# Sequence tails four tokens to a partition, turned by one-hot matmuls, with casts and copies dealt out anew

## The chip, the cores and the metric

The kernel runs on one core of one Trainium2 chip. Five engines take part, each with its own instruction stream: TensorE (matmuls, called PE in the profile, its weight loads PEld), VectorE (DVE), ScalarE (ACT), GpSimd (POOL) and SyncE (SP), whose stream issues all transfers that matter here. Work done by one engine and needed by another is handed over by semaphores. The metric is the device time of one execution in microseconds; three runs of the kernel before took 306.62, 306.86 and 310.41 us, and their median, 306.86, is the time to which the change is compared.

## The reference

Eight sequences of 576 tokens pass through attention with 8 heads of 64 in which a token sees only tokens at most 32 away, and then, all 4608 tokens together, through two layers with a squared rectifier between them:

```python
B, H, S, D = q.shape                                   # 8, 8, 576, 64
scores = np.matmul(q, k.transpose(0, 1, 3, 2)) / np.sqrt(D)
scores = np.where(np.abs(pos[:, None] - pos[None, :]) <= 32, scores, -1e9)
attn = np.exp(scores - np.max(scores, axis=-1, keepdims=True))
attn = attn / (np.sum(attn, axis=-1, keepdims=True) + 1e-09)
x = np.matmul(attn, v).transpose(0, 2, 1, 3).reshape(B * S, H * D)
r = np.maximum(x @ w_in, 0.0)                          # 512 -> 2048
return (s * (r * r) + b) @ w_out                       # 2048 -> 512
```

Inputs and output are float32; the kernel multiplies in bfloat16.

## The kernel before

**Attention.** A sequence has nine tiles of 64 tokens. Two neighbouring tiles make a unit; a unit's scores are taken transposed (keys on partitions, a window of 128 queries beside them), ScalarE takes the exponential out of PSUM, VectorE multiplies by a mask of ones and zeros, and TensorE multiplies by V, to which a column of ones is added for the row sums. `finish` divides (VectorE) and brings the result X into the array `xt`, with the model dimension on partitions: for the first units (number below `XPE`, line 913) by four transposes on TensorE and a copy on ScalarE (line 923), for the later ones by a DMA that transposes, issued on SP (line 932).

**Q and K.** For that, Q and K must lie with head dimension on partitions. For sequences 0 to 2 the first 512 tokens are loaded four tokens to a partition, in runs of 1 KB, cast, and turned on TensorE. The last 64 tokens, the tail ("t"), are loaded apart in `part` (line 701): one token to a partition, Q on partitions 0 to 63 and K on 64 to 127, in runs of 256 bytes, one per token and head. The tail is cast (line 691), turned by four 128x128 transposes (line 705) into a PSUM bank of W, AVN or SC, and two copies on ScalarE (line 696) take Q and K out. Sequences 3 to 7 are loaded by `piece` (lines 752, 759), cast on GpSimd (line 778) and turned by DMA (line 794); they are treated as one long sequence, `LONG`.

**V** is loaded by SP (line 605) and cast at line 614, by GpSimd for sequence 1 and by VectorE from sequence 2 on; sequence 0 has paths of its own (`spread_runs`).

**The layers.** Tokens go through in blocks of 512; `SPLIT` cuts blocks 0, 1 and 2 into smaller ones. `s1` is the first layer: matmuls into one of two halves of PSUM bank W (line 1147), the rectifier on ScalarE (line 1154), the square on VectorE (line 1160). `second` is the second layer of a block in seven products instead of eight (line 1204), for which VectorE forms sums and differences of the weights (line 1176) and of the squared activations (line 1196), and adds up the results (line 1220). `constant` puts the term of b through w_out (line 1279). Weights are loaded in sixteen pieces (line 577) and cast by GpSimd (line 580).

**PSUM** has four banks of two halves here: W, O, SC, AVN. `av_banks` says in which one a unit's attention-times-V and the transposes of its X are put; `late_scores` (lines 984 and 987) takes the scores of sequence 0's last tile, which need the tail.

**What sets the order.** The program is built as a graph of tasks, each with an engine, an estimated cost, a key (due time, small is early) and the buffers that it reads and writes. `plan` goes through it with a model of the engines and of the DMA rings and writes out one fixed order per engine; transfers of the first three sequences and of the weights are chained in the order of `ORDER0`, `ORDER1` and `ORDER2`. So an estimate, a key or an engine that changes can move other tasks, also far away. `stir` (line 659) adds matmuls whose result nobody reads, a number of times by `STIR`.

Of the kernel before, what the change touches and what calls it, by code (L numbers as in the profile page):

```python
# [11 lines left out]
S = 576  # L12
# [19 lines left out]
SPLIT = {0: (224, 128, 160), 1: (256, 256), 2: (256, 256)}  # L32
FIRST = ((0, 0), (1, 0), (0, 1), (2, 0), (1, 1), (2, 1), (0, 2), (1, 2), (2, 2), (0, 3), (1, 3), (2, 3))
WOUTE = (("pool", "pool"),) * 4
# [5 lines left out]
XPE = 25  # L40
# [9 lines left out]
EV0 = ("act", "dve", "act", "dve", "pool")  # L50
BANK1 = ("O", "AVN", "SC", "O", "AVN")
EV1 = ("pool", "pool", "pool", "pool", "pool")
EV2 = ("dve",) * 5
# [3 lines left out]
        ("turn", 3, "q"): 1, ("turn", 3, "k"): 1, ("scores", 2): 1, ("scores", 3): 1, ("av", 0): 5}  # L57
# [266 lines left out]
def bass_sliding_window_symmetric__then__act_starrelu_kernel(  # L324
# [23 lines left out]
    with ExitStack() as es:  # L348
# [332 lines left out]
        def part(b, which, load_key, key, banks, slack):  # L681
# [4 lines left out]
            res, tile = banks[take("bank", len(banks))]  # L686
            tile = tile.bitcast(BF16)
# [11 lines left out]
            if which == "t":  # L699
                stg, stgr = stage(DM)  # L700
                add("sp", [lambda e, src=src, p0=p0: e.dma_start(
                    stg[p0:p0 + 64, :].rearrange("p (h d) -> p h d", h=H), src[b, :, 512:S, :].rearrange("h p d -> p h d"))
                    for src, p0 in ((q, 0), (k, 64))], 1000.0, writes=stgr, key=load_key, dma=("l", 64, 27.0))
                cast(nat[:, 0:DM], stg, DM, stgr)
                add("pe", [lambda e, a=a: e.transpose(tile[:, 128 * a:128 * a + 128], nat[:, 128 * a:128 * a + 128], IDENT[:, :])
                           for a in range(NPAIR)], 300.0, reads=natr + ["IDENT"], writes=[res], key=key)
                view = tile[:, 0:512].rearrange("p (a c) -> p a c", a=NPAIR)
                for name, dst, c0 in (("QT", QT[slot][:, :, WIN + 512:WIN + S], 0), ("KT", KT[slot][:, :, 512:S], 64)):
                    leave(dst, view[:, :, c0:c0 + 64], 256, [(name, slot, NTILE - 1, pr) for pr in range(NPAIR)])
                return  # L710
# [151 lines left out]
        def av_banks(b, u):  # L862
            name = ("SC", "O", "SC", "O", "AVN")[u] if b == 0 else BANK1[u] if b == 1 else "AVN"
# [34 lines left out]
        def finish(b, u, key=None):  # L898
# [14 lines left out]
            if n < XPE:  # L913
# [8 lines left out]
                for a0, a1 in zip(cuts, cuts[1:]):  # L922
                    add("act", lambda e, a0=a0, a1=a1: e.copy(  # L923
                        XT[:, :, a0 % XR:a0 % XR + a1 - a0], view[:, :, p0 + a0 - x0:p0 + a1 - x0]),
                        190 + 0.833 * 4 * (a1 - a0), reads=avr, writes=xt_res(a0, a1), key=key)
# [635 lines left out]
```

## Time and profile before

| what | value |
|---|---|
| median of three runs | 306.86 us |
| the profiled execution | 308.19 us |
| its span, first to last instruction | 306.3 us |
| mean granted TensorE clock | 0.994 |
| busy: TensorE, VectorE, ScalarE, GpSimd | 295.7, 237.2, 157.3, 66.6 us |
| moved by DMA | 54.31 MB |

The span is that of the profiled execution; what lies around it is in that execution's own time. Busy shares are means over stages that have different limits, so the stretches of the span are read one by one. TensorE's matmuls are pipelined: a single matmul's duration holds a drain that overlaps the next one, and what a matmul costs in a row of them is the duration of the row divided by their number.

### The profile page before, as it was taken

To read this page: it belongs to the slowest core of one execution; us is meant where nothing else is said; L and a number is where in the kernel's file an instruction comes from. 1 tells how busy PE (TensorE), PEld (TensorE's weight loads), DVE (VectorE), ACT (ScalarE), POOL (GpSimd) and SP (SyncE) were. 2 spreads that over 40 slices of the span, in tenths; PEclk is the share of its full clock that TensorE was granted. 3 is DMA by queue.
4 is the path that set the end of the run, shared out by engine and by line. 5 is a ranking of instruction groups with operands and counts; after the bars stand their busy time and mean duration, and the time that the engine had idled before them with its cause. 6 is when DMAs were issued, how large, how long until landed. Compare 5 with 4: busy or idle time off the path is not lost.

```text
span 306.3 us, 8830 instructions
## 1 busy us (share of the span) xinstructions
PE 295.7 (97%) x3851; PEld 212.3 (69%) x3851; DVE 237.2 (77%) x409; ACT 157.3 (51%) x246; POOL 66.6 (22%) x78
## 2 busy tenths in 40 slices
PE   8989999899999999999999999998999999999994
PEld 3458777698888887567666675665666666666783
DVE  4666888899879796999799888897867776566673
ACT  3746975684877563655555345543454433333200
POOL 5155577200000360046024400460000000000000
PEclk9979999999999999999999999999999999999999
DMA  7999999999992997999799779997803111200223
GB/s 208 306 254 313 315 287 354 274 260 238 179 216 67 251 209 148 279 234 188 187 242 184 145 178 253 185 169 136 235 20 88 54 47 35 69 34 2 70 72 107
DMA packets 118073, 54.31 MB, mean 177 GB/s; under 512 B 90688, under 2 KB 113856, under 8 KB 118032
## 3 DMA queue, kind: packets, MB, share of 16 engines
q1 hardware_dynamic: 118032, 53.72, 75.6%
q8 instruction: 31, 0.51, 0.8%
q14 instruction: 10, 0.08, 0.1%
HBM read 36.70 MB, written 9.44 MB: 151 GB/s over the span
## 4 chain that ended last, share of the span: by engine, by line
PE 73%; DMA 17%; SPq 3%; POOL 3%; DVE 1%; ACT 1%; issue 0%; POOLq 0%
PE o L1204 31%; PE w L1147 30%; DMA stg<-in_moe_w_out_dram 5%; DMA stg<-in_k_dram 4%; PE avn L884 3%; DMA stg<-in_q_dram 3%; DMA stg<-in_moe_w_in_dram 3%; PE sc L1204 2%; POOL nat L778 2%; SPq L759 2%; PE sc L826 2%; DMA kt<-nat 2%; PE avn L915 1%; POOL wout L580 1%; PE avn L718 1%; ACT ex L1005 1%
## 5 line engine op out<-in xcount | busy, mean ns | idle before, releaser
L1147 PE MATMUL w<-xt,win 128*128 128x512 bf16 (+4 forms) x832 | 144.6, 316 | 0.3 <-issue 0.3
L1154 ACT ACTIVATE r<-w 128x512 bf16<-128x512 f32 (+2 forms) x148 | 86.4, 587 | 97.5 <-PE w L1147 96.0
L1147 PEld LDWEIGHTS w<-xt,win 128*128 128x128 bf16 x832 | 74.9, 99 | 34.4 <-issue 1.3
L1160 DVE TENSOR_TENSOR gt<-r 128x1024 bf16<-128x1024 bf16 (+3 forms) x100 | 62.1, 628 | 23.8 <-ACT r L1154 23.1
L1204 PE MATMUL o<-wout,gt 128*128 128x256 bf16 x528 | 66.4, 273 | 0.0
L1204 PEld LDWEIGHTS o<-wout,gt 128*128 128x128 bf16 x528 | 51.0, 98 | 12.7
L778 POOL CAST nat<-stg 128x1024 bf16<-128x1024 f32 (+2 forms) x28 | 33.8, 1207 | 78.4 <-DMA stg<-in_q_dram 62.4
L854 ACT ACTIVATE ex<-sc 128x1024 bf16<-128x1024 f32 (+1 forms) x29 | 29.7, 1023 | 15.7 <-PE avn L884 13.2
L1204 PE MATMUL o<-tw,gt 128*128 128x256 bf16 x272 | 34.6, 273 | 0.0
L1220 DVE SCALAR_TENSOR_TENSOR outs<-o,sb,cvec 128x512 f32<-128x512 f32 (+1 forms) x36 | 25.8, 717 | 8.1 <-PE o L1204 7.8
L1204 PEld LDWEIGHTS o<-tw,gt 128*128 128x128 bf16 x272 | 26.3, 98 | 7.2
L1220 DVE SCALAR_TENSOR_TENSOR outs<-o,sb,outs 128x512 f32<-128x512 f32 (+1 forms) x27 | 19.2, 713 | 7.1 <-PE o L1204 7.0
L1196 DVE TENSOR_TENSOR gt<-gt 128x1024 bf16<-128x1024 bf16 (+1 forms) x26 | 24.4, 940 | 0.3
L858 DVE TENSOR_TENSOR ex<-ex,mask 128x1024 bf16<-128x1024 bf16 (+1 forms) x29 | 22.1, 762 | 1.5 <-ACT ex L854 0.8
L908 DVE TENSOR_TENSOR xn<-avn,rec 128x512 bf16<-128x512 f32 (+1 forms) x31 | 21.3, 686 | 0.5
L884 PE MATMUL avn<-vb,ex 64*64 64x65 bf16 x944 | 19.9, 197 | 1.4 <-DMA kt<-nat 1.2
L884 PEld LDWEIGHTS avn<-vb,ex 64*64 64x64 bf16 x944 | 12.9, 106 | 10.6 <-issue 5.5
L1204 PE MATMUL o<-tw,gsum 128*128 128x256 bf16 x136 | 17.7, 273 | 0.0
L1204 PEld LDWEIGHTS o<-tw,gsum 128*128 128x128 bf16 x136 | 13.0, 98 | 3.7
L614 DVE CAST vb<-vst 128x512 bf16<-128x512 f32 (+1 forms) x28 | 13.8, 498 | 1.6 <-DMA vst<-in_v_dram 1.6
L1196 DVE TENSOR_TENSOR gsum<-gt 128x1024 bf16<-128x1024 bf16 x18 | 13.6, 758 | 0.3
L923 ACT COPY xt<-avn 128x512 bf16<-128x512 bf16 (+2 forms) x19 | 10.0, 533 | 5.1 <-PE avn L915 5.0
(130 smaller groups left out, 228.6 us busy)
## 6 DMA issues: line engine op xcount, KB each, us to landing
out_dram<-outs SPq DMA_DIRECT2D x32, 256.0 KB, 3.1
vst<-in_v_dram SPq DMA_DIRECT2D x28, 256.0 KB, 4.9
stg<-in_k_dram SPq DMA_DIRECT2D x24, 256.0 KB, 6.7
stg<-in_q_dram SPq DMA_DIRECT2D x5, 1024.0 KB, 6.8
stg<-in_moe_w_in_dram SPq DMA_DIRECT2D x8, 512.0 KB, 8.2
stg<-in_moe_w_out_dram SPq DMA_DIRECT2D x8, 512.0 KB, 7.6
stg<-in_q_dram SPq DMA_DIRECT2D x4, 512.0 KB, 8.4
stg<-in_k_dram SPq DMA_DIRECT2D x4, 512.0 KB, 8.3
```

The costliest lines, as they stand in the source:

```text
L614: (lambda e: e.tensor_copy(VB[0:n, vb, :, 0:D], VST[0:n, vs, :, :])),
L778: (lambda e, dst=dst, src=src: e.tensor_copy(dst, src)),
L854: add("act", lambda e, dst=flat_dst, src=flat_src: e.activation(dst, src, AF.Exp, bias=0.0, scale=0.125), 190 + 0.833 * 512 * len(hs), rea ...
L858: add("dve", lambda e, flat=flat, mask=mask: e.tensor_tensor(flat, flat, mask, ALU.mult), 130 + 0.53 * 512 * len(hs), reads=[("E", ei, hp, ...
L884: return [lambda e: e.matmul(av[64 * x:64 * x + 64, h, 0:D + 1], lhsT=buf[64 * g:64 * g + 64, h % 2, h // 2, c:c + 64], rhs=VB[64 * g:64 * ...
L908: add("dve", lambda e: e.tensor_tensor(XN[xi][0:p1, :].rearrange("p (a c) -> p a c", a=H), av[0:p1, :, 0:D], REC[ri][0:p1, :].rearrange("p ...
L1147: add("pe", [lambda e, g=g, kc=kc: e.matmul(wt[:, g, :], lhsT=WIN_BF[:, kc, (f0 + g) * 128:(f0 + g + 1) * 128], rhs=XT[:, kc, t0 % XR:t0 % ...
L1154: add("act", lambda e: e.activation(rt, wt, AF.Relu, bias=0.0, scale=1.0), 190 + 0.833 * ng * nt, reads=[("W", wb)], writes=[("R1", rb, ha ...
L1160: add("dve", lambda e: e.tensor_tensor(GT[gs][:, f1:f1 + nf, g0:g0 + nt], rr, rr, ALU.mult), 130 + 0.55 * nf * nt, reads=[("R1", rb, x) fo ...
L1196: add("dve", lambda e: e.tensor_tensor(dst, x, y, op), 1240.0 if half is None else 690.0, reads=reads, writes=writes, key=k)
L1204: add("pe", [lambda e, g=g, j=j, dst=dst: e.matmul(dst, lhsT=lhs[:, g, 128 * j:128 * j + 128], rhs=rhs[:, g, :], start=first and g == 0 an ...
L1220: add("dve", lambda e, src=src, dst=dst, other=other: e.scalar_tensor_tensor(dst, src, SB128[:, 0:1], other, ALU.mult, ALU.add), 200 + 1.0 ...
```

## The change

1. The tail's load: its tokens lie four to a partition (partition = head and group of four tokens), Q in the first 256 columns and K in the next, in runs of 1 KB. It is turned by 16 matmuls against columns picked from the identity, each for one of the four tokens or K's four, and one half of the heads, into float32 PSUM; the two copies out undo the order.
2. Engines: from sequence 2 on, V is cast on ScalarE and VectorE in turn, ScalarE first in each sequence. The last piece of w_out is cast by VectorE. Of sequence 0's five copies of X, the second is done by VectorE.
3. Banks and waits of sequence 0: unit 2 uses AVN and not SC, and no longer waits for unit 0's transposes; the late scores use W and not AVN.
4. Three matmuls whose result nobody reads are added behind unit 2's transposes of sequence 0.
5. Block 3 is cut into two halves of 256 tokens.
6. `XPE` is 23 and not 25: two units of X more are turned by DMA.

```diff
-SPLIT = {0: (224, 128, 160), 1: (256, 256), 2: (256, 256)}
+SPLIT = {0: (224, 128, 160), 1: (256, 256), 2: (256, 256), 3: (256, 256)}
-WOUTE = (("pool", "pool"),) * 4
+WOUTE = (("pool", "pool"),) * 3 + (("pool", "dve"),)
-XPE = 25
+XPE = 23
+COPY0 = ("act", "dve", "act", "act", "act")
-EV2 = ("dve",) * 5
+EV2 = ("act", "dve", "act", "dve", "act")
-        ("turn", 3, "q"): 1, ("turn", 3, "k"): 1, ("scores", 2): 1, ("scores", 3): 1, ("av", 0): 5}
+        ("turn", 3, "q"): 1, ("turn", 3, "k"): 1, ("scores", 2): 1, ("scores", 3): 1, ("av", 0): 5, "late": 3}
...
-                add("sp", [lambda e, src=src, p0=p0: e.dma_start(
-                    stg[p0:p0 + 64, :].rearrange("p (h d) -> p h d", h=H), src[b, :, 512:S, :].rearrange("h p d -> p h d"))
-                    for src, p0 in ((q, 0), (k, 64))], 1000.0, writes=stgr, key=load_key, dma=("l", 64, 27.0))
+                add("sp", [lambda e, src=src, c0=c0: e.dma_start(
+                    stg[:, c0:c0 + 256], src[b, :, 512:S, :].rearrange("h (s i) d -> h s (i d)", i=4))
+                    for src, c0 in ((q, 0), (k, 256))], 1000.0, writes=stgr, key=load_key, dma=("l", 16, 50.0))
...
-                add("pe", [lambda e, a=a: e.transpose(tile[:, 128 * a:128 * a + 128], nat[:, 128 * a:128 * a + 128], IDENT[:, :])
-                           for a in range(NPAIR)], 300.0, reads=natr + ["IDENT"], writes=[res], key=key)
+                tile = wide
+                pick = IDENT.rearrange("p (a x s) -> p x a s", a=NPAIR, x=2)
+                add("pe", [lambda e, i=i, hp=hp: e.matmul(
+                    tile[64 * hp:64 * hp + 64, 64 * i:64 * i + 64].rearrange("p (a s) -> p a s", a=NPAIR),
+                    lhsT=nat[:, 64 * i:64 * i + 64], rhs=pick[:, hp, :, :], start=True, stop=True)
+                    for i in range(8) for hp in (0, 1)], 400.0, reads=natr + ["IDENT"], writes=[res], key=key)
...
-            name = ("SC", "O", "SC", "O", "AVN")[u] if b == 0 else BANK1[u] if b == 1 else "AVN"
+            name = ("SC", "O", "AVN", "O", "AVN")[u] if b == 0 else BANK1[u] if b == 1 else "AVN"
...
+                    if n < len(COPY0) and COPY0[n] == "dve":
+                        add("dve", lambda e, dst=dst, src=src: e.tensor_copy(dst, src),
+                            60 + 1.04 * 4 * (a1 - a0), reads=avr, writes=xt_res(a0, a1), key=key)
...
-                        AVN[0:64, hp, pr * 128:pr * 128 + 128], lhsT=KT[0][p, pr, 64 * x:64 * x + 64],
+                        W[0:64, hp, pr * 128:pr * 128 + 128], lhsT=KT[0][p, pr, 64 * x:64 * x + 64],
...
-                land["av", 0, u] = pe_part(-25.0 + u, av=av_part(0, u), waits=[land["xt", u - 2]] if u > 1 else [])
+                land["av", 0, u] = pe_part(-25.0 + u, av=av_part(0, u), waits=[land["xt", u - 2]] if u > 2 else [])
                 finish(0, u, -25.0 + u)
+            stir("late", ("SC", 0), SC[:, 0, :], EARLY + 0.45, [land["xt", 2]])
```

More of the change, by code (lines that the diff above doesn't have):

```diff
@@ L685, in part @@
             nat, natr = NAT[ni], [("NAT", ni)]
-            res, tile = banks[take("bank", len(banks))]
-            tile = tile.bitcast(BF16)
+            res, wide = banks[take("bank", len(banks))]
+            tile = wide.bitcast(BF16)
             eng, out_eng = FCAST[which] if b < 2 else "act", FOUT[which]
```

21 lines of the change are left out of this document (11 added, 10 removed).

## The prediction

> **What bounds the kernel now.** I read the page's head first, then the same span cut into stretches (columns: stretch, its length, busy time of TensorE, its weight loads, VectorE, ScalarE and GpSimd with counts, granted TensorE clock, DMA share, GB/s).
>
> ```profile
> span 306.3 us, 8830 instructions
> PE 295.7 (97%) x3851; PEld 212.3 (69%) x3851; DVE 237.2 (77%) x409; ACT 157.3 (51%) x246; POOL 66.6 (22%) x78
> 6.00:20.00 14.00, 12.13 (x210) 6.30 (x208) 8.10 (x15) 8.36 (x15) 4.24 (x6) 0.99 1.12 300
> 20.00:24.00 4.00, 3.92 (x72) 3.14 (x70) 2.85 (x5) 2.54 (x6) 2.28 (x3) 0.60 1.18 213
> 24.00:55.00 31.00, 29.64 (x571) 24.10 (x571) 24.57 (x47) 22.06 (x41) 20.86 (x22) 1.00 1.10 316
> 55.00:58.00 3.00, 2.05 (x21) 1.40 (x19) 1.86 (x4) 1.57 (x3) 1.11 (x2) 1.00 1.15 273
> 58.00:205.00 147.00, 147.00 (x2087) 109.64 (x2085) 128.61 (x212) 87.19 (x130) 34.43 (x30) 1.00 0.98 203
> 205.00:210.00 5.00, 3.84 (x35) 2.06 (x35) 3.84 (x6) 1.83 (x4) 0.00 (x0) 1.00 0.97 188
> 210.00:302.30 92.30, 92.20 (x885) 64.24 (x885) 63.75 (x103) 31.84 (x50) 0.00 (x0) 1.00 0.25 71
> ```
>
> The reader is to see two kernels in one. From 58 us TensorE is full: 147.00 of 147.00, 3.84 of 5.00, 92.20 of 92.30. Before 58 us it isn't: it lacks 14.00 − 12.13 = 1.87, 0.08, 1.36 and 0.95 us, and between 20 and 24 us it had 0.60 of its clock. There the DMA share is above 1 in every stretch. So the first 58 us are held by what the DMA engines bring and by the chains from it to TensorE; after that, only TensorE's own work counts, and one gap near 208 us. All that this change can win lies in about 4 us of early idle time, the slow stretch, and that gap. The waits of TensorE name two of them:
>
> ```profile
> PE avn L884 <- DMA kt<-nat: 1.2, 1, 1.2
> PE sc L1279 <- POOL wout L580: 1.0, 1, 1.0
> 19.00:20.00 1.00, 0.84 (x24) 0.54 (x21) 0.07 (x1) 1.00 (x4) 0.75 (x1) 0.90 1.12 199
> 20.00:21.00 1.00, 0.92 (x41) 0.66 (x36) 0.00 (x0) 1.00 (x3) 0.29 (x1) 0.50 1.07 214
> 23.00:24.00 1.00, 1.00 (x23) 0.86 (x24) 0.96 (x3) 0.43 (x2) 0.49 (x1) 0.89 1.15 195
> ```
>
> The last three rows show the clock fall to 0.50 late in the microsecond from 19 and come back within the one from 23: about 0.2 + 3 + 0.2 = 3.4 us at half clock, behind a stretch in which TensorE idled. That costs up to 1.7 us.
>
> **The start: sequence 0 (clock, bank and copy edits).** The timeline there (start, duration, engine, line; in brackets the idle time before):
>
> ```profile
> 18.56 0.40 PE L705 MATMUL w<-ident,nat 128*128 128x128 bf16 x4 [0.76 <-POOL nat L691]
> 19.89 0.62 ACT L923 COPY xt<-o 128x512 bf16<-128x512 bf16 x1
> 20.07 0.94 PE L884 MATMUL sc<-vb,ex 64*64 64x65 bf16 x32
> 20.37 1.44 ACT L997 ACTIVATE ex<-avn 64x1024 bf16<-64x1024 f32 x2
> 20.95 2.79 PE L1147 MATMUL w<-xt,win 128*128 128x224 bf16 x16
> 21.07 0.21 DVE L906 RECIPROCAL rec<-sc 128x8 f32<-128x8 f32 x1 [2.00 <-PE sc L884]
> 26.52 0.93 PE L1147 MATMUL w<-xt,win 128*128 128x224 bf16 x8
> ```
>
> TensorE waits 0.76 us for the tail's cast, and only later runs unit 2's attention-times-V (0.94 us), since that shares bank SC with unit 0. In bank AVN, and without the wait for unit 0's transposes, it can run inside the 0.76. Unit 1's copy (0.62 on ScalarE, ahead of the exponentials) goes to VectorE, idle for 2.00 us just then, so the late exponentials (1.44) may begin up to 0.62 sooner. Against that, the late scores move from AVN to W, the bank of the first layer: its first matmuls, now begun at 20.95 beside the exponentials, must wait for their end. That is the wait added; behind it on TensorE stands everything of the first layer, and ScalarE and VectorE wait for that in turn. The exponentials end at 20.37 + 1.44 = 21.81, or 21.2 with the copy gone: a start 0.25 to 0.9 later. The 16 matmuls took 2.79 at half clock; at full clock, from 0.93 for eight, about 1.7. So they would end between 21.2 + 1.7 = 22.9 and 21.8 + 1.7 = 23.5 where they ended at 23.74: 0.2 to 0.8 won if the clock holds, up to 0.9 lost if it doesn't. With the attention already done elsewhere I take **−0.6** (ends −1.7 and +0.9).
>
> The three added dummy matmuls, by the five of line 659 below, take 3 × 0.22 = 0.65; they are to fall in the wait for bank W, so most is hidden: **+0.1** (0 to 0.65 if that cover is gone).
>
> **The tails.** One tail is 128 KB of Q and 128 KB of K. The rows are of the timeline, of a stretch, and of the DMA issues (KB each, us to landing):
>
> ```profile
> 14.55 1.25 PE L659 MATMUL sc<-onesw 128*128 128x512 bf16 x5
> 25.00:30.00 5.00, 5.00 (x78) 4.32 (x70) 3.11 (x7) 3.36 (x8) 2.48 (x3) 1.00 1.11 344
> stg<-in_q_dram SPq DMA_DIRECT2D x8, 128.0 KB, 5.3
> 47.87 0.40 PE L1279 MATMUL sc<-wout,onesw 128*32 128x512 bf16 x4
> 28.88 0.61 PE L718 MATMUL avn<-ident,nat 128*128 128x128 bf16 x8
> ```
>
> Now they come in runs of 256 bytes, afterwards of 1 KB. The trace has no row for one form alone; the nearest are two stretches with the DMA full, one in which sequence 1's tail is under way (213 GB/s, 20 to 24 us), one mostly of long runs (344, from 25 us). 262 KB take 1.23 us at the one and 0.76 at the other: 0.47 a tail, 0.94 for the two tails that ORDER0 and ORDER1 issue ahead of the last w_out load. SP also waits for free staging, so not all of it arrives: **−0.4** (ends −0.9 and 0, below it in the first rival). SP issues two transfers per tail, as now.
>
> On TensorE, 16 one-hot matmuls of 64 columns replace 4 transposes, which took 0.40 with their drain (18.56 us above). Four of 32 weight columns and 512 run in 0.40, not four times that: column halves run side by side. Eight pairs of 64 columns then stream in 8 × 0.03 = 0.2, within the same 0.4; one after the other it is 0.6. I take +0.1 a tail, **+0.3** (0 to +0.75). ScalarE's two copies out move as many elements and stay.
>
> **The last w_out piece.** It is cast by VectorE, not GpSimd. Three rows of the timeline, and one of the groups for the new price:
>
> ```profile
> 56.08 1.04 POOL L580 CAST wout<-stg 128x1024 bf16<-128x1024 f32 x1 [1.01 <-DMA stg<-in_moe_w_out_dram]
> 57.15 2.36 DVE L1176 TENSOR_TENSOR tw<-wout 128x2048 bf16<-128x2048 bf16 x2 [1.14 <-POOL wout L580]
> 57.17 0.40 PE L1279 MATMUL sc<-wout,onesw 128*32 128x512 bf16 x4 [0.95 <-POOL wout L580]
> L691 DVE CAST nat<-stg 128x1024 bf16<-128x1024 f32 x2 | 1.4, 694 | 1.2 <-DMA stg<-in_k_dram 1.2
> ```
>
> 1.04 becomes 0.69, and TensorE waited for its end: **−0.35**. VectorE idles 1.14 there, so nothing is queued behind it; if it were late, squares of the first layer would wait. Only 0.95 can be won here by all terms together, unless TensorE itself arrives earlier, which the first part provides.
>
> **Block 3 in halves, V casts, two units by DMA.** Rows of the chain that ended last (start, duration), of the groups by form (count, busy and mean, idle before), of two lines of DMA issues, and of the timeline:
>
> ```profile
> 65.32 0.87 PE w L1147 x8
> 120.24 0.86 PE w L1147 x4
> L1160 DVE TENSOR_TENSOR gt<-r 128x1024 bf16<-128x1024 bf16 x48 | 37.1, 774 | 18.6 <-ACT r L1154 18.1
> L1160 DVE TENSOR_TENSOR gt<-r 128x512 bf16<-128x512 bf16 x36 | 18.5, 524 | 3.4 <-ACT r L1154 3.3
> L614 DVE CAST vb<-vst 128x512 bf16<-128x512 f32 x26 | 13.0, 505 | 1.6 <-DMA vst<-in_v_dram 1.6
> L668 ACT CAST nat<-stg 128x512 bf16<-128x512 f32 x1 | 0.6, 618 | 1.6 <-DMA stg<-in_q_dram 1.6
> L932 SPq DMA_TRANSPOSE xt<-xn x14: 1181/1259/3060, 175.0 to 245.8; - x14
> 168.11 1.78 SPq L794 DMA_TRANSPOSE kt<-nat  x1
> DMA to landing us min/median/max: 2.3/4.6/6.5
> 176.41 0.40 PE L826 MATMUL sc<-qt,kt 64*64 64x128 bf16 x16
> ```
>
> Eight matmuls of 256 take 0.87, four of 512 take 0.86: 16 such groups, +0.16 on TensorE. VectorE squares 16 × 0.524 − 8 × 0.774 = +2.2 us, ScalarE the same elements. Of 28 V casts 16 go to ScalarE: VectorE −8.1, ScalarE +9.9. Between 58 and 205 us VectorE has 147 − 128.6 = 18 us free, ScalarE 60, and TensorE is full: **0**. A cast that waits for its load would hold the rectifiers queued behind it on ScalarE, and TensorE with them; VectorE waited 1.6 us for such loads in all, and that is the bound.
>
> Two units lose 4 matmuls of 128 each on TensorE, 8 × 0.05 (eight transposes took 0.61 above, four 0.40) = −0.4, and ScalarE two copies. With the split's +0.16, **−0.25**. They add two DMA transposes to SP, 1.26 to 3.06 us each, ahead of sequence 6's loads and transposes. Sequence 6's main K transpose, issued at 168.11, lands 4.6 later by the median, 172.7, and is used at 176.41: 3.7 of cover for 2 × 1.26 = 2.5. So nothing, in my sum; the gap near 208 us is fed by sequence 7, 30 us on, and I leave it at its 1.2 (it may close or double).
>
> **Sum.** −0.6 + 0.1 − 0.4 + 0.3 − 0.35 − 0.25 = −1.2 us. The profiled execution took 308.19 (306.33 of span, 1.86 around it) and would take 307.0. The median of the runs shown is 306.86, 1.33 below the profiled one; I can't see whether those runs had the slow stretch at all, so I count half of the −0.6: 306.86 − 0.9 = 306.0. **I forecast 306.0 us**, 305.2 to 306.6 for this case.
>
> **Rivals.**
>
> *Half the engines.* The new source runs over 8 heads, then 16 groups of four tokens; if the transfer is dealt out by the outer 8, it uses 8 engines, at half of 344 GB/s: 262 KB take 1.52 us, 0.29 worse than now. For two tails +0.6 in place of −0.4: 307.0. For it: nothing in the trace shows a load with an outer count of 8. Against it: other engines' packets overlap. [...] Chance 0.2.
>
> *SP is late for sequence 6 (slower).* If the two X transposes cost SP the longest seen, 2 × 3.06 = 6.1, the 3.7 of cover fails and TensorE stands 2.4 us at 176: 306.0 + 2.4 = 308.4. It decides from 1.85 us a transpose. For it: one of 14 took 3.06, and SP's loads there wait on a full DMA. Against: the median of 1.26. Chance 0.2.
>
> *The clock.* The half-clock stretch stays or moves behind the wait for bank W: +0.9 in place of the counted −0.3: 307.2. For it: the first layer begins later. [...] Chance 0.15.
>
> *Both gaps close.* The start gains 1.7 in place of 0.3 and 208 us its 1.2: 303.4 at best, 304.5 at half of it. Chance 0.1.
>
> **How the numbers follow.** Forecast 0.35. The range takes in the rivals: 304.2 (half of the best case) to 308.9 (the late transposes with some of the clock's loss). Two per cent, about what a measurement of this kernel tells from no change, is 6 us: below 300.7 no case lies, above 313.0 only an order of queues gone wrong in several places. Faster 0.01, within 0.96, slower 0.03.
>
> **What would show it.** The clock row at 1.00 from 20 to 24 us; first-layer matmuls starting past 21.2; the wait at line 1279 under 0.6; tail loads landing sooner than the 5.3 of their row; 16 matmuls of a tail in 0.4 to 0.6; VectorE near 231 us and ScalarE near 167; no new TensorE wait near 176. A new TensorE wait of over a microsecond after 58 us would make me wrong, as would tails landing later.

## The result and the profile after

The changed kernel took 308.02 us (median of 22 runs, 307.15 to 310.35), the kernel before 306.64 (22 runs beside them on the same chip, 305.03 to 311.31). The ratio is 1.0052 with a 95% interval of 1.0033 to 1.0070; when the changed kernel was run again on another chip (median 308.56, there against 307.68) it was 1.0030 [1.0002, 1.0058]. Weighted by the two intervals that is 1.0045, or 1.4 us slower. The forecast was 306.0, a gain of 0.9. The ratios here and below compare undisturbed runs alone (all or nearly all of a kernel's, but nine of twelve and six of twelve for two of the kernels with sixteen groups outermost, whose other runs took 313.8 to 315.3), so they needn't be the quotient of two medians. A tenth of a per cent is 0.31 us.

The profiled execution after took 307.18 us. The page's head:

```profile
span 305.4 us, 9028 instructions
PE 291.9 (96%) x3924; PEld 217.1 (71%) x3946; DVE 236.1 (77%) x403; ACT 164.1 (54%) x259; POOL 63.9 (21%) x77
```

The stretches (their length, busy time of TensorE, its weight loads, VectorE, ScalarE, GpSimd, granted clock, DMA share, GB/s):

```profile
6.00:20.00 14.00, 11.50 (x240) 5.92 (x238) 8.69 (x17) 7.88 (x14) 3.89 (x6) 1.00 1.09 307
20.00:24.00 4.00, 3.53 (x72) 2.11 (x68) 2.75 (x6) 2.67 (x5) 2.56 (x4) 1.00 1.10 272
24.00:55.00 31.00, 28.80 (x543) 24.05 (x544) 25.30 (x47) 21.67 (x40) 20.48 (x22) 1.00 1.06 318
55.00:58.00 3.00, 2.87 (x39) 1.96 (x38) 3.00 (x5) 2.39 (x6) 0.00 (x0) 1.00 1.07 274
205.00:210.00 5.00, 4.95 (x35) 3.20 (x33) 4.46 (x7) 2.33 (x4) 0.87 (x2) 1.00 0.96 184
```

In this execution three losses of before are gone: the clock is 1.00 from 20 to 24 us (it was 0.60), the gap at the w_out wait is nearly closed (2.87 of 3.00, where it was 2.05), and so is the gap near 208 us (4.95 of 5.00, where it was 3.84). But TensorE now lacks 2.50, 0.47 and 2.20 us in the first three stretches, where it lacked 1.87, 0.08 and 1.36. TensorE's waits (in total, times, longest):

```profile
PE w L708 <- POOL nat L692: 1.2, 1, 1.2
...
PE avn L920 <- DVE xn L913: 1.0, 1, 1.0
...
PE o L889 <- POOL vb L615: 0.9, 1, 0.9
```

The wait for the tail's cast grew from 0.76 to 1.2 us, and the waits for K at 208 us (1.2) and for w_out (1.0) have gone, but one for X near 142 us (1.0) and one for a cast of V near 44 us (0.9) have come. In this pair of executions, what was won was given back elsewhere. The wait for the tail's cast is a poor measure of the two kernels, though: it was 2.0 us in a second trace of the changed kernel, and 1.8 and 2.5 in two traces of a kernel that has before's order on TensorE (only w_out's last cast is moved, below).

The two profiled executions are a poor pair for the size of it: before's was 1.55 us above its kernel's median and had the stretch of half clock, after's is 0.84 below its own and hasn't. In one execution of the changed kernel the second layer began at 59.96 us and in another at 61.34, so what follows goes by ratios of many runs for the size, and by traces for the place. The clock of the profiled pair isn't that of the mean either: the granted clock, as the mean over the span, was 0.9940 over 152 executions of the kernel before, 0.9933 over the 22 of the changed kernel and 0.9939 over 12 more. On the mean the change won nothing of it.

### The profile page after: what moved, and what is told of

Its sections match the earlier page's. It is cut to its first block, busy times and chain, and to the rows that moved or that the text cites. A ratio compares the mean times of both kernels' runs of the same rounds, so it can differ in the third digit from the quotient of the medians.

```text
span 305.4 us, 9028 instructions
## 1 busy us (share of the span) xinstructions
PE 291.9 (96%) x3924; PEld 217.1 (71%) x3946; DVE 236.1 (77%) x403; ACT 164.1 (54%) x259; POOL 63.9 (21%) x77
## 4 chain that ended last, share of the span: by engine, by line
PE 83%; DVE 5%; DMA 4%; SPq 3%; ACT 2%; issue 2%; POOL 1%; POOLq 0%
PE w L1157 37%; PE o L1214 34%; PE avn L889 4%; PE sc L831 2%; PE sc L1214 2%; DMA stg<-in_moe_w_in_dram 2%; DMA stg<-in_k_dram 2%; DVE gt L1170 1%; SPq L651 1%; PE avn L920 1%; DVE gsum L1206 1%; SPq L621 1%; SPq L578 1%; ACT r L1164 1%; DVE gt L1206 1%
## 5 line engine op out<-in xcount | busy, mean ns | idle before, releaser
L1157 PE MATMUL w<-xt,win 128*128 128x256 bf16 (+4 forms) x874 | 139.7, 301 | 2.5 <-issue 1.0
L1157 PEld LDWEIGHTS w<-xt,win 128*128 128x128 bf16 x896 | 80.6, 98 | 31.3 <-issue 1.0
L1170 DVE TENSOR_TENSOR gt<-r 128x512 bf16<-128x512 bf16 (+3 forms) x108 | 65.6, 614 | 25.8 <-ACT r L1164 24.8
L783 POOL CAST nat<-stg 128x1024 bf16<-128x1024 f32 (+2 forms) x28 | 32.4, 1158 | 82.4 <-DMA stg<-in_q_dram 67.9
L889 PE MATMUL avn<-vb,ex 64*64 64x65 bf16 x976 | 20.6, 197 | 0.4
L1206 DVE TENSOR_TENSOR gsum<-gt 128x1024 bf16<-128x1024 bf16 x18 | 15.0, 832 | 0.3
L911 DVE RECIPROCAL rec<-avn 128x8 f32<-128x8 f32 (+1 forms) x32 | 6.5, 202 | 8.9 <-PE avn L889 8.9
```

The source lines that it names most:

```text
L783: (lambda e, dst=dst, src=src: e.tensor_copy(dst, src)),
L889: return [lambda e: e.matmul(av[64 * x:64 * x + 64, h, 0:D + 1], lhsT=buf[64 * g:64 * g + 64, h % 2, h // 2, c:c + 64], rhs=VB[64 * g:64 * ...
L1157: add("pe", [lambda e, g=g, kc=kc: e.matmul(wt[:, g, :], lhsT=WIN_BF[:, kc, (f0 + g) * 128:(f0 + g + 1) * 128], rhs=XT[:, kc, t0 % XR:t0 % ...
L1170: add("dve", lambda e: e.tensor_tensor(GT[gs][:, f1:f1 + nf, g0:g0 + nt], rr, rr, ALU.mult), 130 + 0.55 * nf * nt, reads=[("R1", rb, x) fo ...
L1206: add("dve", lambda e: e.tensor_tensor(dst, x, y, op), 1240.0 if half is None else 690.0, reads=reads, writes=writes, key=k)
```

## The experiments

Each ratio is to the kernel before on the same chip, from 6 to 22 executions. Profiles are quoted by the line numbers of each kernel, which lie within ten of those above.

**Each suspect alone.** First block 3's split, taken out of the changed kernel and put alone into the kernel before:

```diff
-SPLIT = {0: (224, 128, 160), 1: (256, 256), 2: (256, 256), 3: (256, 256)}
+SPLIT = {0: (224, 128, 160), 1: (256, 256), 2: (256, 256)}
```

> The changed kernel with block 3 whole again, all else kept. Theory S (the halves of block 3 make VectorE the bound near 142 us: 16 squares of 512 columns in place of 8 of 1024, each held longer while GpSimd casts): TensorE's 1.0 us wait for VectorE's division near 142 us goes, the time falls by about 1 us below the changed kernel, to about 1.002 of the kernel before. Theory T (the tails' new form costs the time, in the first 25 us): no difference to the changed kernel, 1.005. Theory L (the loss is spread in the early order of queues): no difference either.

> The kernel before with block 3 in halves and nothing else. Theory S: a wait of TensorE for VectorE appears in the stretch in which block 3's squares run, 1 us or more since VectorE has all V casts here too; 1.003 to 1.006 of the kernel before. Theories T and L: within 0.1% of the kernel before.

Measured 1.0056 [1.0025, 1.0086] without it, and 1.0078 [1.0041, 1.0115] with it alone. The stretch from 138 to 146 us of the changed kernel:

```profile
138.00:146.00 8.00, 6.98 (x120) 5.70 (x122) 7.90 (x13) 4.45 (x8) 3.75 (x4) 1.00 1.09 177
```

The same stretch without the split:

```profile
138.00:146.00 8.00, 8.00 (x103) 5.31 (x101) 7.04 (x12) 5.30 (x9) 4.44 (x4) 1.00 0.94 162
```

And in the kernel before, as it is and with the split alone:

```profile
138.00:146.00 8.00, 8.00 (x147) 5.53 (x145) 7.69 (x12) 4.52 (x8) 5.06 (x4) 1.00 0.95 179
138.00:146.00 8.00, 7.13 (x150) 5.75 (x148) 7.96 (x14) 3.54 (x6) 4.57 (x5) 1.00 1.13 198
```

With the split VectorE is busy for 7.90 or 7.96 of 8 us and TensorE stands for about a microsecond; without it VectorE has 7.04 or 7.69 and TensorE is full. So in these two kernels the wait comes and goes with the split. The split isn't needed for it, though: with block 3 whole, the new tail alone has a wait of 0.8 us for X's division at 146 us, and the early half below one of 1.5 us at 145. Nor did taking the split out of the changed kernel lower the time measurably, so it is not what the whole change costs.

The new tail alone, in the kernel before (its load, the cast as it was, the 16 matmuls and the copies out, as in the diff of the change):

```diff
-                    stg[p0:p0 + 64, :].rearrange("p (h d) -> p h d", h=H), src[b, :, 512:S, :].rearrange("h p d -> p h d"))
+                    stg[:, c0:c0 + 256], src[b, :, 512:S, :].rearrange("h (s i) d -> h s (i d)", i=4))
...
```

> The kernel before with the tails in their new form (load four tokens to a partition, one-hot matmuls) and nothing else. Theory T: each tail load runs on half of the DMA engines, the loads behind it on those engines come later, 1.003 to 1.006. My prediction's step: 0.1 to 0.6 us faster, 0.998 to 1.000. Theories S and L: within 0.1% for the tail by itself, but the early order may move it by 0.3% either way.

Measured 1.0102 [1.0073, 1.0130], the dearest single edit. One early stretch of it:

```profile
15.00:31.00 16.00, 12.89 (x235) 8.84 (x234) 8.92 (x18) 6.13 (x12) 7.93 (x9) 0.68 1.06 296
```

The same stretch of the kernel before:

```profile
15.00:31.00 16.00, 14.48 (x280) 11.03 (x278) 9.86 (x21) 9.74 (x21) 8.40 (x9) 0.89 1.12 284
```

And of the changed kernel:

```profile
15.00:31.00 16.00, 13.81 (x305) 10.35 (x303) 10.12 (x21) 9.36 (x19) 8.43 (x9) 1.00 1.07 302
```

Alone, the new tail leaves TensorE idle for 3.1 of 16 us, and the clock granted is 0.68 (10 us at half speed). This isn't one execution's chance: the mean granted clock of the twelve is 0.9847, against before's 0.9940, and 0.0093 of a span of 306 us is 2.8 us, an estimate of the most that the clock can have cost, of the 3.1 us lost. With the start's edits beside the tail TensorE idles less, and in this execution of the changed kernel the clock holds; in its second trace the same stretch has 0.79.

**Eight outermost or sixteen.** In the changed kernel's trace each tail load's semaphore has 8 increments as the load lands (and one 1.0 to 1.7 us after the issue), where each of before's had 16. That 8 engines then carry the load, as the first rival supposed, was the author's reading; no trace shows a packet's engine. To price the 8, groups of tokens instead of heads were put outermost, with the columns of the identity picked to match:

```diff
-                    stg[:, c0:c0 + 256], src[b, :, 512:S, :].rearrange("h (s i) d -> h s (i d)", i=4))
+                    stg[:, c0:c0 + 256], src[b, :, 512:S, :].rearrange("h (s i) d -> s h (i d)", i=4))
-                pick = IDENT.rearrange("p (a x s) -> p x a s", a=NPAIR, x=2)
+                pick = IDENT.rearrange("p (s a x) -> p x a s", a=NPAIR, x=2)
```

It was run in the changed kernel, in the changed kernel without the split, and alone in the kernel before:

> The changed kernel with its tails dealt out with the sixteen groups of four tokens as outer count and the 8 heads inside (and the picked columns to match); the order of all instructions is the same. Theory T: the tails land up to 0.5 us sooner, and the time falls by 0.5 to 1.2 us, to 1.001 to 1.003. Theories S and L: the tails land sooner but the time stays within 0.1% of the changed kernel, since something else ends last.

> The changed kernel with its tails over sixteen outer groups and block 3 whole. Theory S and T together: the late part 240.5 us in place of 241.5, the early part some tenths shorter, so 0.998 to 1.001 of the kernel before. Theory L (the early order of queues costs it): the late part 240.5, but 1.002 to 1.004.

> The kernel before with the tails in their new form, dealt over sixteen outer groups. Against the run with 8 heads outside (1.010). Theory T: the half of the engines is the cost; falls to 1.000 to 1.003. Theory L: the new plan that the cheaper tail gives, with the old banks and waits of sequence 0, is the cost: stays at 1.007 to 1.012.

Measured 1.0009 [0.9974, 1.0045], 1.0091 [1.0061, 1.0121] and 1.0086 [1.0042, 1.0130], where the same kernels with eight heads outermost gave 1.0052 and 1.0030, 1.0056, and 1.0102. Twice a little better, once worse: how the load is dealt out makes no difference to the whole time that these runs can tell. It does to a landing. From the issue of the tail's K load to the last increment of its semaphore, sequence 1's tail took 9.4 to 11.1 us in eight traces with eight increments, 8.5 to 9.8 in the three with sixteen and 7.7 to 9.6 in nine with the old tail. Sequence 0's, for which TensorE waits, hardly differs: 5.7 to 7.1, 5.6 to 6.5 and 5.9 to 7.9.

**The changed kernel again, and the start's edits alone.** The second has item 3, item 4 and the copy on VectorE of item 2 in the kernel before:

```diff
-            name = ("SC", "O", "SC", "O", "AVN")[u] if b == 0 else BANK1[u] if b == 1 else "AVN"
+            name = ("SC", "O", "AVN", "O", "AVN")[u] if b == 0 else BANK1[u] if b == 1 else "AVN"
...
+            stir("late", ("SC", 0), SC[:, 0, :], EARLY + 0.45, [land["xt", 2]])
```

> The changed kernel itself, unaltered, on the chip of the runs beside it: about 1.005 of the kernel before, whatever the theory. Its use is a second trace: from the first matmul of the second layer to the last one 241.5 us as in the first trace if that part is fixed by the order (theory S), while the time up to that first matmul may differ by a microsecond between executions.

> The kernel before with the edits of sequence 0 alone: unit 2 in AVN without its wait, late scores in W, the second copy of X on VectorE, three dummy matmuls; tails as before. My prediction's step: 0.5 us faster, 0.997 to 1.000. Theory L: the bank W is held by the late scores and the first layer waits, 1.001 to 1.005.

The first gave 1.0030, told above. The start's edits alone gave 1.0025 [0.9995, 1.0055]: no gain, where −0.6 us (0.998) was forecast. In its trace the clock is 1.00 throughout, but TensorE waits 0.6 us for the late exponentials in bank W and 1.5 us for w_out, where it waited 0.95 in before.

**The wait for the tail's cast.** Same order on TensorE, another engine for the cast; and, separately, the tail loaded ahead of the first quarter of w_in:

```diff
-FCAST = {"q0": "pool", "k0": "dve", "t": "pool", "q1": "pool", "k1": "dve"}
+FCAST = {"q0": "pool", "k0": "dve", "t": "dve", "q1": "pool", "k1": "dve"}
```

```diff
-ORDER0 = ("va", "vb", "w0a", "t", "w0b", "w1a", "v4", "w1b")
+ORDER0 = ("va", "vb", "t", "w0a", "w0b", "w1a", "v4", "w1b")
```

> The changed kernel with the tails of sequences 0 and 1 cast on VectorE instead of GpSimd; TensorE's order is unaltered. In the changed kernel TensorE waits 1.2 us (2.0 us in its repeat) for GpSimd's cast of sequence 0's tail, right behind which the turn's 16 matmuls stand. Theory C (the wait for that cast is what the new tail costs): the wait goes to 0.3 or less, the first first-layer matmul comes 0.8 to 1.5 us earlier than 21.75 us, and the time falls by 0.8 to 1.5 us, to a ratio of 1.000 to 1.002 to the kernel before. Theory D (the landing of the load sets it: the cast of 512 columns takes about 0.5 us of the wait, the rest is DMA): the wait shrinks by 0.3 us at most or is renamed to a DMA, ratio 1.003 to 1.006. Rival: what is gained ahead of the second layer is taken back at the waits there, same ratio with an earlier first-layer start.

> The changed kernel with sequence 0's tail loaded ahead of the first quarter of w_in instead of behind it. Theory A (the tail's arrival is what costs): the tail lands 1 to 2 us sooner, the wait of 1.2 us for GpSimd's cast ahead of the tail's turn goes, the time falls by 0.7 to 1.5 us, ratio 0.998 to 1.002. Rival B (something else stands behind it: w_in lands later and the first-layer matmuls wait for its cast, or the work that the start's edits put ahead of the first layer sets its start): the wait goes or changes its name, ratio 1.002 to 1.006.

Measured 1.0061 [1.0025, 1.0097] and 1.0084 [1.0050, 1.0118]. TensorE's wait for the tail with the cast on VectorE:

```profile
PE w L708 <- DVE nat L692: 1.0, 1, 1.0
```

And with the tail loaded first:

```profile
PE w L708 <- POOL nat L692: 1.2, 1, 1.2
...
PE w L1157 <- DVE xt L930: 1.1, 1, 1.1
```

The first keeps a wait of 1.0 under another engine's name, which points to the landing of the load and not to the engine. The second has the tail 1.83 us sooner (its cast at 15.82 us, not 17.65), but the planner moved the turn forward with it, so the same 1.2 stands ahead of it, and the first layer now waits 1.1 us for X. Loading the tail earlier was no remedy.

**Both suspects out.** The changed kernel with the old tail, and then also with block 3 whole:

```diff
-                    stg[:, c0:c0 + 256], src[b, :, 512:S, :].rearrange("h (s i) d -> h s (i d)", i=4))
+                    stg[p0:p0 + 64, :].rearrange("p (h d) -> p h d", h=H), src[b, :, 512:S, :].rearrange("h p d -> p h d"))
...
```

> The changed kernel with the old tail load and the four transposes; all other edits stay. Theory T2 (the tail's new shape is what costs, through the early stretch): 1.000 or less, the TensorE wait for GpSimd's cast gone or below 0.6 us, tail of sequence 0 landing 7 us after its issue. Theory S (the split of block 3 costs 0.5 to 1 us at the TensorE wait near 142 us, the tail nothing): ratio stays at 1.003 to 1.006 and that wait of 0.9 us stays.

> The changed kernel with the old tail and with block 3 whole: left of the change are the start's edits, the casts of V on ScalarE, the last cast of w_out on VectorE, and XPE. If tail and split are the two costs (T2 and S), this is the fastest of all: ratio 0.994 to 0.999, late part 240.5 us, no wait near 142 us. If neither is, it stays at 1.002 to 1.006.

Measured 1.0048 [1.0007, 1.0090] and 1.0016 [0.9972, 1.0060]. With both out the loss can no longer be told from nothing, but the gain that was expected isn't seen either. With the old tail alone put back, TensorE's wait for the tail's cast falls to 0.2 us, and the time stays: that wait is not what the change costs.

**The change in two halves.** The early half is tail and start's edits; the late half is split, casts of V, XPE and w_out; between them stands a run of the late half without the split:

```diff
-WOUTE = (("pool", "pool"),) * 4
+WOUTE = (("pool", "pool"),) * 3 + (("pool", "dve"),)
-XPE = 25
+XPE = 23
-EV2 = ("dve",) * 5
+EV2 = ("act", "dve", "act", "dve", "act")
```

> The kernel before with three edits of the change: later casts of V alternating between ScalarE and VectorE, XPE 23, and the last cast of w_out on VectorE. By the prediction's terms: w_out -0.35, V casts 0, XPE -0.4, together -0.75 us, ratio 0.9975 (0.996 to 0.999), with the TensorE wait for w_out under 0.6 us and the gap near 208 us smaller. Rival (these terms are given back at other waits, as 1.2 us of the late part in the start-only run): 1.000 to 1.004.

> The late half alone: the kernel before with block 3 split, casts of V alternating, XPE 23 and the last cast of w_out on VectorE; old tail, old start. Theory L (the late half costs it, by VectorE's squares behind GpSimd's casts): ratio 1.004 to 1.008, a TensorE wait for xn near 142 us of about 1 us, late part 241.5 us or more. Theory E: 0.998 to 1.002.

> The early half of the change alone: the kernel before with the new tail load and turn and the start's edits, and none of split, casts of V, XPE or w_out. Theory E (the early half costs it: TensorE waits for the tail's cast in sequence 0, and the gains of the start do not pay for it): ratio 1.004 to 1.008, first first-layer matmul at 21.5 to 24.5 us, late part within 0.5 us of 241.05 us. Theory L (the late half costs it): 0.998 to 1.002.

Measured 1.0004 [0.9969, 1.0039] for the late edits without the split, 1.0009 [0.9977, 1.0041] for the late half, and 1.0049 [1.0023, 1.0075] for the early half. The early half alone costs as much as the whole change. Two waits of the late half:

```profile
PE avn L884 <- DMA kt<-nat: 1.5, 2, 0.8
...
PE sc L1279 <- DVE wout L580: 0.9, 1, 0.9
```

Its stretch from 138 to 146 us:

```profile
138.00:146.00 8.00, 8.00 (x158) 6.71 (x156) 7.91 (x12) 4.99 (x9) 5.58 (x5) 1.00 1.21 173
```

With half of V's casts off VectorE, TensorE is full from 138 to 146 us in spite of the split (VectorE is as busy as with the split alone, 7.91 of 8 us); but the waits for K and w_out are back. The early half's waits:

```profile
PE o L889 <- issue: 2.1, 1, 2.1
...
PE w L708 <- POOL nat L692: 0.6, 1, 0.6
```

And the stretch behind the first of them:

```profile
47.00:50.00 3.00, 3.00 (x26) 2.71 (x25) 2.31 (x6) 1.62 (x3) 2.23 (x3) 0.51 1.05 387
```

Here the wait for the tail is small. TensorE stops for 2.1 us, up to 46.73 us, in the middle of a row of attention matmuls, and a stretch at half clock follows. The other long wait stands near 145 us, as in the kernels with the split, though block 3 is whole here:

```profile
145.21 0.40 PE L920 MATMUL avn<-ident,xn 128*128 128x128 bf16 x4 [1.49 <-DVE xn L913]
```

This execution took 311.10 us, 1.6 above the median of its kernel, so the two waits tell where the early half can lose, not how much.

**GpSimd's casts beside VectorE's squares.** The casts of Q and K of sequences 4 to 7, in the changed kernel, on ScalarE:

```diff
-CASTE = {"q": "pool", "k": "pool"}
+CASTE = {"q": "act", "k": "act"}
```

> The changed kernel with the casts of q and k of the sequences from the fourth to the last (28 instructions, 32.4 us of GpSimd) on ScalarE. Theory P (GpSimd's casts hold VectorE's bf16 operations; a square of 512 takes 0.41 us alone and 0.86 us beside such a cast): the mean of the squares of 512 falls to 0.42 to 0.45 us over 95 to 210 us, the wait for xn near 142 us goes, VectorE's busy time falls by 8 us or more. In the total: -0.5 to -1 us against the changed kernel if ScalarE's 28 us more hold nobody; the rival is that ScalarE's casts of 1.04 us stand ahead of the ReLUs in its queue and TensorE waits for r, 0.3 us each time: +1 to +3 us.

Measured 1.0081 [1.0049, 1.0113], slower. The groups of VectorE's squares in the changed kernel (count, busy and mean, idle before):

```profile
L1170 DVE TENSOR_TENSOR gt<-r 128x1024 bf16<-128x1024 bf16 x40 | 30.3, 757 | 20.2 <-ACT r L1164 20.1
L1170 DVE TENSOR_TENSOR gt<-r 128x512 bf16<-128x512 bf16 x52 | 26.4, 511 | 4.4 <-ACT r L1164 3.7
```

Its stretch from 95 to 210 us:

```profile
95.00:210.00 115.00, 112.77 (x1638) 85.60 (x1647) 97.69 (x154) 63.15 (x97) 32.42 (x28) 1.00 0.96 199
```

The same groups with the casts on ScalarE:

```profile
L1170 DVE TENSOR_TENSOR gt<-r 128x1024 bf16<-128x1024 bf16 x40 | 27.6, 690 | 23.2 <-ACT r L1164 23.0
L1170 DVE TENSOR_TENSOR gt<-r 128x512 bf16<-128x512 bf16 x52 | 22.2, 433 | 10.1 <-ACT r L1164 10.0
```

The same stretch, and then a wait of TensorE:

```profile
95.00:210.00 115.00, 113.30 (x1645) 85.22 (x1644) 85.14 (x153) 85.29 (x124) 0.00 (x0) 1.00 0.94 196
```

```profile
PE w L1157 <- ACT r L1164: 1.5, 2, 1.2
```

That GpSimd's casts hold VectorE is shown: without GpSimd's 32.42 us of casts VectorE does the same work in 12.6 us less, and the wait near 142 us is gone. The gain isn't: ScalarE has 22 us more, and TensorE waits 1.2 us for its rectifier instead.

**One edit that gains.** The last cast of w_out on VectorE, alone in the kernel before, run on two chips:

```diff
-WOUTE = (("pool", "pool"),) * 4
+WOUTE = (("pool", "pool"),) * 3 + (("pool", "dve"),)
```

> The kernel before with the last cast of w_out on VectorE alone. The prediction's term: -0.35 us, the TensorE wait of 0.95 us for w_out falling to 0.6 or less, ratio 0.9989 (0.997 to 1.000). Rival (the second layer's start is set by the first-layer matmuls ahead of it, so nothing is won): 1.000 to 1.003.

> The kernel before with the last cast of w_out on VectorE alone, unaltered from the run only_wout. If the gain is real: 0.995 to 0.9985, the wait of 0.95 us for w_out gone and no TensorE wait above 0.5 us after 60 us. If it was chance: 0.9985 to 1.002.

Measured 0.9970 [0.9936, 1.0003] and 0.9966 [0.9931, 1.0001]: each interval still just holds 1, and weighted together, 0.9968 [0.9944, 0.9992], they don't. That is 1.0 us faster than the kernel before, and it beats both kernels. Its orders on TensorE, ScalarE and SP are those of before; one cast changes its engine. The head of TensorE's waits in its second trace:

```profile
PE w L705 <- POOL nat L691: 1.8, 1, 1.8
...
PE w L1147 <- ACT r L1154: 0.3, 2, 0.2
```

And the timeline at the place of before's gap near 208 us:

```profile
206.21 1.89 PE L1147 MATMUL w<-xt,win 128*128 128x512 bf16 x7
208.13 0.32 PE L884 MATMUL avn<-vb,ex 64*64 64x65 bf16 x16
```

Both the wait for w_out and the gap near 208 us are gone, and behind 58 us no wait of over 0.3 us has come in their place; so it is in the first trace too. The wait for the tail's cast is longer in these executions (2.5 and 1.8) than in before's (0.8).

## Why the prediction was wrong

The time lay inside the range (306.64 × 1.0052 = 308.2, of 304.2 to 308.9), and "within 2%" was right; the sign was wrong. By halves, in microseconds (a ratio less 1, times 307.7):

| part | forecast | measured |
|---|---|---|
| early half (start, dummies, tail load, one-hot) | −0.6 | +1.5 [+0.7, +2.3] |
| w_out alone | −0.35 | −1.0 [−1.7, −0.2] |
| rest of the late half (split, V casts, XPE) | −0.25 | +1.3 [0.0, +2.5], late half less w_out |
| the whole | −1.2 (−0.9 counted) | +1.4 [+0.9, +1.9] |

Three steps failed: the start's gain, by the clock and by an overlap; the time that the tail's load was to save; and the cover on VectorE for the split and the casts of V. Where in the early half its +1.5 us lies is shown only in part.

**What bounds the kernel**: right. Early transfers and chains until 58 us, TensorE after; but "TensorE is full" after 58 us was read as if nothing could open a gap there, and most of the edits, early ones too, opened or closed one.

**The start, −0.6 (counted at half): the first step that failed.** Alone its edits measured +0.8 [−0.2, +1.7]. The gain was to come from the clock, 2.79 us for sixteen matmuls against 1.7, less a later start. It was read from one execution, 1.55 us above its kernel's median, and on the mean the clock stayed as it was (0.9940 before; 0.9933 and 0.9939 after). That the execution profiled had 1.00 from 20 to 24 us was luck. The overlap failed as well; the timeline of the changed kernel answers that of before:

```profile
18.32 0.44 PE L708 MATMUL w<-ident,nat 128*64 128x64 bf16 x16 [1.20 <-POOL nat L692]
18.69 0.72 PE L889 MATMUL avn<-vb,ex 64*64 64x65 bf16 x32
...
20.15 1.42 ACT L1006 ACTIVATE ex<-w 64x1024 bf16<-64x1024 f32 x2
...
20.68 0.81 PE L660 MATMUL sc<-onesw 128*128 128x512 bf16 x3
...
21.75 0.94 PE L1157 MATMUL w<-xt,win 128*128 128x224 bf16 x8
```

Unit 2's attention-times-V was to run inside the wait for the tail. The order puts it behind the tail's turn (18.69), so it hides nothing of that wait (here 1.20). The late exponentials begin 0.22 sooner (20.15, before 20.37), not 0.62, and the first layer 0.80 later, at 21.75, as said: "starting past 21.2". So the loss that was priced came, and what was to pay for it, the clock on the mean and the overlap, didn't. The dummies (+0.1) cost no more than that: their 0.81 lies beside the exponentials that bank W waits for.

**The tails, −0.4 and +0.3: the load's step failed.** The turn's size was right: the 16 matmuls take 0.44 (forecast 0.4 to 0.6). That the loads come sooner isn't borne out. The row of the 128-KB loads of Q says 3.8 us, in place of 5.3, but it holds eight loads, three of them tails, and the profile gives no landing for a load that lands in 8 increments: the 3.8 is that of the others. The tails' own landings, Q and K, from the start of the issue, in the kernel before and in the changed kernel with sixteen groups outermost:

```profile
DMA to landing us min/median/max: 6.2/7.7/9.2
...
DMA to landing us min/median/max: 4.7/6.4/8.6
```

With eight, by the increments told above, sequence 1's lands later than before's and sequence 0's hardly sooner. Sequence 0's tail on GpSimd's timeline in the changed kernel:

```profile
17.65 0.61 POOL L692 CAST nat<-stg 128x512 bf16<-128x512 f32 x1 [0.86 <-POOL win L581]
```

It is cast at 17.65 where it was cast at 17.89: 0.24 sooner, though its K load was issued 0.54 sooner (11.05 us for 11.59), and with TensorE there earlier still. A rate of transfer, from two stretches in which other loads run too, was turned into time on the path without looking whose load is on the path. What the new tail costs is told by its runs: 3.1 us alone, up to 2.8 of it by the clock (the estimate above), and 0.7 more than the start's edits when it stands beside them (+1.5 and +0.8, with intervals that overlap). The wait for its cast isn't the cost: another engine or place for it did not win it back, the early half had only 0.6 of it in its profile, and with the old tail in the changed kernel it was 0.2 and the time the same.

**w_out, −0.35:** the mechanism was right, and the size lies inside what was measured, −1.0 [−1.7, −0.2]. In both of its traces the gap near 208 us is closed too; why a cast 150 us earlier should close it wasn't tried, and before's gap is known from one trace alone. Inside the whole change the wait is gone too, but other waits take its place.

**Split and V casts, 0: wrong.** "VectorE has 18 us free between 58 and 205 us" is a mean over a stretch in which it has none where it matters. The timeline of GpSimd, VectorE and TensorE around the new wait:

```profile
136.09 5.85 POOL L783 CAST nat<-stg 128x1024 bf16<-128x1024 f32 x5 [2.41 <-DMA stg<-in_k_dram]
137.60 1.25 DVE L1170 TENSOR_TENSOR gt<-r 128x512 bf16<-128x512 bf16 x1
...
142.77 0.37 DVE L1170 TENSOR_TENSOR gt<-r 128x512 bf16<-128x512 bf16 x1
143.06 0.68 DVE L913 TENSOR_TENSOR xn<-avn,rec 128x512 bf16<-128x512 f32 x1
...
143.79 0.40 PE L920 MATMUL avn<-ident,xn 128*128 128x128 bf16 x4 [1.02 <-DVE xn L913]
```

Beside a run of GpSimd's casts a square of 512 takes 1.25 us, 0.37 after it. Cutting a block in halves makes 16 squares of 512 out of 8 of 1024, and beside a cast one of 512 lost 0.45 us on the mean and one of 1024 0.41 (0.86 for 0.41, 1.09 for 0.69, in before's trace). My mean of 0.524 had such cases in it, but spread over the kernel. Sharing out V's casts may help against it: the split alone costs 0.78%, and in the late half, where they are shared out, 0.05% (1.0009 with it, 1.0004 without, each within 0.35%). But they are shared out in the changed kernel too, and the wait is there. It comes with the new tail and block 3 whole as well, and in the run with Q's and K's casts off GpSimd it is gone, split and all. So the split is neither needed for it nor, without those casts, enough. VectorE's busy time came to 236.1 (forecast near 231) and ScalarE's to 164.1 (near 167).

**XPE, −0.4,** wasn't tried alone. Sequence 6 was not late, so that rival fell: near 176 us TensorE goes from the second layer to the attention without a wait.

```profile
174.94 1.91 PE L1214 MATMUL o<-tw,gt 128*128 128x256 bf16 x16
176.78 0.32 PE L889 MATMUL avn<-vb,ex 64*64 64x65 bf16 x16
```

In the late half, which has the same edit, it was late by a little: TensorE waits 0.8 us for K up to 176.70. Of the other rivals, *half the engines* had its 8 increments for 16 and a later landing of sequence 1's tail, but that 8 engines carry it at half of the rate (its 1.52 us) is shown by no run, and the whole time didn't tell 8 from 16; *the clock* came true in most executions, as it did before the change; of *both gaps close* the two closed in the execution profiled, and the gain was given back at 17, 44 and 142 us. One slip of the sums: half of that best case is 306.0 − 1.3 = 304.7, not 304.5, nor the 304.2 at which the range begins.

**What stays open.** Which single edit of the early half carries its +1.5 us: alone, the tail costs 3.1 us and the start's edits 0.8 [−0.2, +1.7], together 1.5, and the changed kernel with the old tail was no faster (1.0048). What TensorE waits for in the 2.1 us of "issue" in the early half's profile. A candidate is V of sequence 1: the changed kernel's wait of 0.9 at that place is for its cast, and between 40 and 50 us matmuls with V wait 0.3 to 2.1 us in seven of the eight traces with the eight-increment tail, and in nine with the old tail 0.3 at most, but for one of 0.8. No run changes that load alone. And how much of each number is the planner's new order rather than the edit's own cost: only with w_out alone, the tail's cast on VectorE and the sixteen groups outermost was TensorE's order left as it was.

## What to carry to other kernels

Busy time free over a long stretch is no cover: look at the stretch in which the operation will stand, and at who is next to it there. Before taking a gain from a slow place of one profiled execution, compare that execution's own time with the median of its kernel; if it lies well above, that place may not be there in the others. Where the mean clock of every execution is listed, it tells whether a change holds the clock; one trace doesn't. And in a kernel ordered by a planner, an edit that leaves the order alone (one cast, one engine) is worth trying alone before six together: of three such edits here one won, and none of the other runs did.

## What the runs showed of the hardware

**VectorE beside GpSimd.** VectorE's squares (bfloat16, SBUF to SBUF) take longer while a GpSimd cast runs: those of 512 took 0.37 to 0.43 us without a cast beside them (0.41 on the mean of 27 in before's trace, 0.42 of 41 in after's) and 0.86 (of 9) and 0.87 (of 11) with one, up to 1.26. The two of 1.25 us near 138 and 140 us in the changed kernel end 0.27 and 0.28 us after the cast beside them ends. X's division, which reads float32 from PSUM, takes 0.69 us either way (in before's trace 686 ns over 21 without a cast beside them and 687 over 10 with one; 686 over 28 with no late GpSimd casts at all).

**The stretches of half clock.** In the kernel with the new tail alone, the half-clock stretch has these rows around it:

```profile
20.00:21.00 1.00, 0.59 (x19) 0.44 (x19) 0.00 (x0) 0.86 (x4) 0.92 (x1) 0.88 1.00 245
21.00:30.00 9.00, 7.74 (x123) 5.59 (x122) 5.13 (x11) 3.59 (x6) 5.00 (x6) 0.50 1.09 310
30.00:31.00 1.00, 1.00 (x12) 1.00 (x11) 0.33 (x1) 0.00 (x0) 0.35 (x1) 0.50 0.89 287
```

0.24 + 9 + 1 = 10.2 us, and in before 3.4. The changed kernel had such a stretch in the execution profiled when it was run again:

```profile
18.00:19.00 1.00, 0.00 (x0) 0.00 (x0) 0.40 (x1) 0.00 (x0) 0.59 (x1) 0.71 1.16 249
19.00:25.00 6.00, 5.85 (x85) 3.54 (x86) 2.61 (x5) 3.10 (x6) 3.61 (x5) 0.50 1.08 282
25.00:26.00 1.00, 0.99 (x22) 0.65 (x20) 0.00 (x0) 0.22 (x1) 0.53 (x1) 0.88 1.10 321
```

0.58 + 6 + 0.24 = 6.8 us, behind a microsecond in which TensorE did nothing. The early half's has 0.51 from 47 to 50 us (told above) and 0.77 in the microsecond behind: 2.94 + 0.46 = 3.4 us. So the four lasted 3.4 us twice, 6.8 and 10.2, each behind a stretch in which TensorE idled in part. It hadn't idled all the while: in the 3.4 us ahead of them it was busy for 2.31 us (before), 1.67 (new tail alone), 1.89 (changed kernel, second trace) and 1.07 (early half). Nor did idling always bring one: with the tail loaded first TensorE was busy for only 12.10 of the 16 us from 15 to 31, with waits of 1.24 and 1.09 us among the idle time, and the clock was 1.00. With the start's edits, their three dummy matmuls among them, the stretch from 15 to 31 us kept its clock (1.00) in the profiles of the changed kernel and of the early half, though not in the changed kernel's second; the tail costs 1.02% alone, and tail and start's edits together 0.49%.
